# One written order for all engines in a four-layer attention kernel: keys' features in three steps, rows normalised two segments ahead

## The chip, the cores and the metric

The kernel runs on one core of a Trainium2 chip. The metric is the device time of one execution in microseconds (us), lower is better. A core has five engines that take their instructions in order, each from its own queue: TensorE (PE in the profile; PEld is its weight load), VectorE (DVE), ScalarE (ACT), GpSimd (POOL), and SyncE (SP), which here only starts transfers (DMAs). They wait for each other by semaphores, which the compiler sets where one instruction reads what another has written, or takes over its buffer.

## The reference, cut

Four layers of two kinds, A, B, A, B, over 2048 rows of 512 numbers, 32 heads of 16. Each layer is `x + layer(layernorm(x))`, and both layers of a kind share their weights.

```python
def _A_ref(x, wqkv, w_phi, wo):                    # linear attention
    q, k, v = heads(x @ wqkv)
    phi = lambda u: concat(softmax(u @ w_phi), softmax(-(u @ w_phi)))   # per head, 16 -> 32
    kv, z = sum_s phi(k)[s] v[s], sum_s phi(k)[s]
    o = phi(q) kv / (phi(q) z + 1e-6)
    return o @ wo

def _B_ref(x, wq, wk, wv, wo, beta):               # four segments of 512 rows
    for s in range(4):
        a_dot = causal_softmax(q_s k_s^T / 4) v_s
        a_mem = phi(q_s) M / (phi(q_s) z + 1e-6)   # phi(t) = t + 1 if t > 0 else exp(t)
        o_s = g * a_mem + (1 - g) * a_dot          # g = sigmoid(beta)
        M, z = M + phi(k_s)^T v_s, z + sum phi(k_s)
    return o @ wo
```

## The kernel before

**Products.** Everything is float32. The large products run on TensorE in three matmuls each: both operands are split into a rounded part `hi` and a rest `lo`, and hi*hi, hi*lo and lo*hi are summed (`mm3`, L418). So a product of 128 rows with a 512x512 matrix is 12 matmuls into a tile of 128x512 in PSUM, the accumulators' memory. Such tiles come from a pool `g` of three buffers; two larger ones, `lg` and `mx`, have one buffer each.

**A linear layer (A)** has two passes. `pass1` (L639) goes through four segments of 512 rows in the order 1, 2, 3, 0 (`SEGS`). For a segment:

- `norm_T` (L391) loads four tiles of rows, computes their moments on DVE (`moments`, `guard`), the inverse root on ACT by Ln and Exp (`root`) and sharpens it in six small instructions (`refine`, on DVE, or on POOL where `off` is set); ACT normalises each tile in place (`normal`), and `columns` transposes it on TensorE, ACT copying `hi` and DVE subtracting `lo`. With `slow` this is a generator of 15 steps, 11 of them up to the last normalisation.
- `v_tile` (L476) makes the values: four tiles, each a projection (12 matmuls) and a copy on ACT.
- `kproj` (L663), one for each of four tiles of keys: a projection, ACT's copy of it, then the features: largest and smallest of each head (`extremes`, DVE), differences to them (two instructions on POOL, `differences`), `exp` on ACT, sums, reciprocal and half of a scaling on DVE, the other half on POOL (`scale_k`). These differences, and the weights of the keys, already contain `w_phi`.
- `qproj` (L677): a projection, its copy, extremes, and a store; the features are made in the second pass.
- `kv` (L695): 32 matmuls add features-times-values of two tiles into `kva`, in buffer `lg` for tiles 0 and 1, `mx` for 2 and 3.

In segment n the loop at L735 takes a step of `k0 q0 k1 q1 v0 k2 q2 k3 q3 v1` and then one of `side`: the next segment's `norm_T`, then its values. Features of a key tile are all issued at once, behind its projection. In the last segment, features are issued in separate steps (L747 to L771). `pass2` (L781) computes the queries' features, products with `kva`, the division and the output projection with a residual, 16 tiles.

**The first layer** also has `first` (L572), which loads weights, multiplies `w_phi` into them on TensorE (`folded`) and makes segment 1's `norm_T` far enough that its rows are normalised; and beside its `pass1` runs `prepare` (L299, driver L1250), which splits 20 pieces of layer B's and output weights (a load, casts on ACT, subtractions on POOL) and stores both parts in DRAM (`kept`), from where `load_w` and `bring` (L235) read them later, two transfers of 1 MB for each matrix.

**A softmax layer (B)** is `steps` (L1114): a loop over numbered steps, with tables written by hand (`FIRST`, `GAPS`, `LAST`, `FINAL`, and `BEFORE` for the steps ahead of the first segment) that say at which step which projection, transposition, load or piece of another layer is issued. `opening` (L1096) loads the first weights and rows and sets constant rows of the operand tiles (`start`, L832, four fills); the driver (L1256) interleaves it with the first 76 steps (`A20`) of the linear layer's second pass before it. The rest of that pass is handed to `steps` as `side`, up to an amount of TensorE work `LEFT`. Layer 2's `steps` takes in turn the beginning of layer 3's `pass1` as `after`: the first segment's rows and values in the table `LAST`, and at L1226 to L1233 three steps of its first key projections, while layer 2's last tiles are added up (`end`, L1085).

**What sets the order.** The program is written by generators; what a scheduler then makes of it depends on flags. Instructions of DVE, ACT, POOL and SP go through `Ordered`, matmuls and transpositions through `held`:

```python
                j = (ends if ordered[0] or back[0] else floor).get(self.engine)
                if j is not None:
                    behind(i, j)
...
        if strict[0] and last[0] is not None:
            behind(i, last[0])
```

`behind` fixes that one instruction follows another on its engine without a wait. With `ordered` and `strict` set, an engine takes its instructions as written: so in `first`, in the last segment of each `pass1` and through the second pass and `steps`. Elsewhere, in segments 0 to 2 of `pass1` and at the very end of `steps`, a scheduler orders instructions within what the data allow, by its own forecast of the time.

Of the kernel before, what the change touches and what calls it, by code (L numbers as in the profile page):

```python
# [15 lines left out]
D = 512  # L16
# [21 lines left out]
LEFT = 44000  # L38
BEGIN = -31
MAXIMA = -9  # L40
A20 = 76
PREP = 6
EVERY = (2, 2)
# [57 lines left out]
          -18: "n", -17: "v2 n", -16: "n", -15: "n n", -14: "q1 n", -13: "n", -12: "v3 n", -11: "n", -10: "k1 n",  # L101
# [4 lines left out]
def interleave_kernel(ctx, tc, x_in, a_wqkv, a_wphi, a_wo, b_wq, b_wk, b_wv, b_wo, b_beta,  # L106
# [25 lines left out]
    strict = [False]  # L132
    last = [None]
    ordered = [False]
    back = [False]
    ends = {}
    floor = {}
    put_off = [None]

# [13 lines left out]
    class Ordered:  # L153


# [3 lines left out]
        def __getattr__(self, op):  # L159
            f = getattr(self.engine, op)  # L160

            def call(*a, **k):
                i = f(*a, **k)  # L163
# [9 lines left out]
    def held(i):  # L173

        if strict[0] and last[0] is not None:
            behind(i, last[0])
# [122 lines left out]
    def prepare():  # L299


        for _ in range(PREP):
            yield
        back[0] = True
        constants()
        back[0] = False
        for m, src in enumerate((b_wq, b_wk)):
            for kc in range(NC):
                raw = T2("xr", 3)
                sync.dma_start(out=raw, in_=src[kc * P : (kc + 1) * P, :])  # L310
                hi = T2("oh", OO, F32R)
                lo = T2("ol", OO, F32R)
                for e in range(2):
                    for r in range(2):
                        rv = raw.rearrange("p (c f r e d) -> p e r c d f", c=NC, f=2, r=2, e=2)[:, e, r]
                        hv = hi.rearrange("p (c f e d r) -> p e r c d f", c=NC, e=2, f=2, r=2)[:, e, r]
                        lv = lo.rearrange("p (c f e d r) -> p e r c d f", c=NC, e=2, f=2, r=2)[:, e, r]
                        back[0] = True
                        act.copy(hv, rv)
                        back[0] = False  # L320
                        pool.tensor_tensor(out=lv, in0=rv, in1=hv.bitcast(F32), op=SUB)
# [972 lines left out]
```

## Time and profile before

| | |
|---|---|
| median of 3 runs | 1601.99 us (1600.36 to 1604.97) |
| the profiled execution's own time | 1601.45 us |
| its span, from first to last instruction | 1599.7 us |
| TensorE busy with matmuls | 1512.0 us, 95% of the span |
| DVE / ACT / POOL busy | 1135.5 / 786.5 / 642.9 us (71% / 49% / 40%) |
| mean granted clock of TensorE | 0.989 of full speed |
| moved by DMA | 195.70 MB, mean 122 GB/s |

Every line of the trace says at what time (us from the span's start) which engine ran what, written as `out<-in` by the tiles' names. Matmuls stand at L185 and transpositions at L189, all recorded instructions of the other engines at L163, since helpers issue them: so they are told apart by tiles. Names in the first passes: `x` rows, `st` their statistics, `xr` and `oh`/`ol` the weights of `prepare`, `hh`/`hl` the columns, `g` a projection's accumulator, `U` a key projection's copy, `tb` a query's, `mm` extremes, `P` (or `e`) features, `es` their sums, `mx` and `lg` the accumulators of `kv`, `v` the values. In a row of one instruction or a run of like ones, the first number is its start, the second its duration together, `xN` their count, and what stands in brackets is the idle time before and what ended it. In a table of windows the columns are the window, its length, the busy time of PE, PEld, DVE, ACT and POOL with the number of instructions, the granted clock, and the mean busy share and GB/s of the DMA engines. A clock of 0.5 means that matmuls take twice as long.

### The profile page before, as it was taken

What the parts mean: (1) busy time and instruction counts of PE and PEld (TensorE: products, weight loads), DVE (VectorE), ACT (ScalarE), POOL (GpSimd) and SP (SyncE); (2) the same over time, 40 slices, a digit from 0 to 9 for tenths busy, and PEclk for the clock granted to TensorE, in tenths of its full rate; (3) what the DMA queues carried; (4) which work ended last, traced back from release to release, by engine and by line L of the source; (5) the groups of instructions that cost most, each with busy time, mean ns of one, the idle gap of its engine ahead of it and who ended that gap; (6) DMA issues with size and microseconds to landing.
All of it is one profiled execution on the core that took longest, in us unless ns stands there. A gap on an engine that the chain in (4) does not pass through costs nothing.

```text
span 1599.7 us, 28160 instructions
## 1 busy us (share of the span) xinstructions
PE 1512.0 (95%) x9856; PEld 1079.1 (67%) x9856; DVE 1135.5 (71%) x3282; ACT 786.5 (49%) x1178; POOL 642.9 (40%) x976
## 2 busy tenths in 40 slices
PE   7999998988999999999999999889889999999998
PEld 6788887765666666666568888777656666666554
DVE  4675775667787887888655657647688778777784
ACT  5444333425565565555534424343455655655553
POOL 1457653413443453433222337433234444533422
PEclk9999999999999999999999999999999999999999
DMA  7348144634443543543232111743354344334331
GB/s 273 132 137 264 73 163 151 185 95 148 132 106 100 140 100 106 140 105 122 81 144 61 52 58 51 236 152 106 103 176 113 103 137 106 102 111 107 81 88 52
DMA packets 100988, 195.70 MB, mean 122 GB/s; under 512 B 13552, under 2 KB 26992, under 8 KB 97776
## 3 DMA queue, kind: packets, MB, share of 16 engines
q1 hardware_dynamic: 99696, 193.38, 40.3%
q8 instruction: 79, 1.29, 0.3%
q10 hardware_dynamic: 1152, 0.52, 0.1%
q14 instruction: 61, 0.50, 0.1%
HBM read 101.05 MB, written 39.85 MB: 88 GB/s over the span
## 4 chain that ended last, share of the span: by engine, by line
PE 67%; DVE 17%; ACT 5%; issue 5%; DMA 3%; POOL 2%; SPq 1%; DVEq 0%; ACTq 0%; POOLq 0%
PE g L185 39%; DVE mx L163 9%; PE mx L185 8%; PE lg L185 8%; PE pv L185 6%; PE g L189 6%; ACT P L163 2%; ACT tb L163 2%; DVE mxs L163 2%; POOL P L163 1%; DVE ta L163 1%; DMA x<-x 1%; DVE es L163 1%; DMA xr<-in 1%; ACT x L163 1%
## 5 line engine op out<-in xcount | busy, mean ns | idle before, releaser
L163 DVE CUSTOM_DVE_ANT_0 mx<-mx,mask 128x128 f32<-128x128 f32 (+3 forms) x1024 | 510.4, 498 | 166.0 <-PE mx L185 131.4
L163 ACT ACTIVATE P<-lg 128x1024 f32<-128x1024 f32 x320 | 328.7, 1027 | 185.6 <-PE lg L185 172.7
L163 POOL TENSOR_SCALAR_AFFINE_SELECT P<-P 128x256 f32<-128x256 f32 (+1 forms) x448 | 190.3, 439 | 439.3 <-ACT P L163 437.6
L185 PE MATMUL g<-hh,wqk 128*128 128x512 f32 x512 | 180.6, 407 | 1.8 <-ACT hh L163 1.3
L185 PE MATMUL mx<-e,e 63*128 63x256 f32 (+2 forms) x1024 | 155.6, 360 | 22.0 <-DVE mxs L163 15.8
L185 PE MATMUL lg<-e,e 64*128 64x256 f32 (+2 forms) x1024 | 168.6, 387 | 8.0 <-ACT P L163 7.1
L185 PE MATMUL g<-w,oh 128*128 128x512 f32 x512 | 172.7, 420 | 3.6 <-ACT oh L163 2.7
L185 PE MATMUL pv<-P,v 128*32 128x512 f32 (+3 forms) x2048 | 165.2, 441 | 0.0
L185 PEld LDWEIGHTS lg<-e,e 64*128 64x128 f32 x1024 | 81.2, 184 | 103.6 <-issue 53.8
L185 PE MATMUL g<-w,hh 128*128 128x512 f32 x448 | 145.9, 406 | 3.1 <-ACT tb L163 3.1
L163 DVE DVE_READ_ACCUMULATOR2_ANT mxs<- 128x1 f32 x1024 | 144.5, 141 | 0.0
L185 PEld LDWEIGHTS mx<-e,e 63*128 63x128 f32 x1024 | 82.9, 185 | 70.4 <-DVE mxs L163 49.8
L185 PEld LDWEIGHTS pv<-P,v 128*32 128x32 f32 x2048 | 53.6, 109 | 98.7 <-issue 88.1
L185 PEld LDWEIGHTS g<-hh,wqk 128*128 128x128 f32 x512 | 96.3, 188 | 23.2 <-ACT hh L163 1.8
L185 PEld LDWEIGHTS g<-w,oh 128*128 128x128 f32 x512 | 91.7, 194 | 26.8 <-ACT oh L163 4.1
L163 POOL TENSOR_SCALAR tb<-tb 128x512 f32<-128x512 f32 x48 | 71.5, 1489 | 84.7 <-ACT tb L163 84.7
L185 PE MATMUL g<-w,ol 128*128 128x512 f32 x256 | 103.3, 404 | 1.1 <-DVE ol L163 1.1
L185 PE MATMUL g<-hl,wqk 128*128 128x512 f32 x256 | 100.3, 392 | 0.4 <-DVE hl L163 0.4
L163 ACT CAST ta<-g 128x512 fp32r<-128x512 f32 x64 | 37.4, 585 | 119.4 <-PE g L185 116.4
L185 PEld LDWEIGHTS g<-w,hh 128*128 128x128 f32 x448 | 80.0, 189 | 22.2 <-ACT tb L163 5.2
L185 PE MATMUL g<-w,hl 128*128 128x512 f32 x224 | 88.5, 395 | 0.0
L163 POOL TENSOR_TENSOR P<-P,rr 128x512 f32<-128x512 f32 x32 | 34.6, 1082 | 127.3 <-DVE rr L163 127.3
(133 smaller groups left out, 2714.3 us busy)
## 6 DMA issues: line engine op xcount, KB each, us to landing
e<-ta SPq DMA_DIRECT2D x384, 128.0 KB
wqk<-wqk SPq DMA_DIRECT2D x64, 512.0 KB
x<-x SPq DMA_DIRECT2D x48, 256.0 KB
xr<-in SPq DMA_DIRECT2D x28, 256.0 KB
pq<-tb SPq DMA_DIRECT2D x24, 256.0 KB
tb<-pq SPq DMA_DIRECT2D x24, 256.0 KB
x<-xr SPq DMA_DIRECT2D x24, 256.0 KB
xr<-x SPq DMA_DIRECT2D x24, 256.0 KB
```

What stands on the lines that cost most here:

```text
L163: i = f(*a, **k)
L185: return held(nc.tensor.matmul(*a, **k))
L189: return held(nc.tensor.transpose(*a))
```

## The change

It gives every engine one written order from the first instruction to the last, and rewrites what the scheduler had ordered:

- **Order.** `Ordered` and `held` always tie an instruction to the one written before it on its engine; the flags `ordered`, `strict`, `back` and `floor` are gone.
- **First passes, keys.** In segments 0 to 2 the steps are `k0 k1 q0 q1 k2 v0 k3 q2 q3`, and the features of a key tile are issued in three parts: extremes and differences behind its own projection, exp a projection later, the scaling another one later. `kv(1)` of a segment is issued behind `k0` of the next one (`late`).
- **Rows.** `upcoming(n)` opens the `norm_T` of segment n, always `slow` and with `refine` on POOL. In segment n, the side work is: the columns of segment n + 1, its values, then the rows of segment n + 2 up to their normalisation (`rows`, 11 steps).
- **Second `pass1`.** The queries' weights (`awq`) are loaded from the fifth step on, no longer behind the first segment's keys; side work waits until layer 2 has ended, and the features of the keys that are projected before that are put in a list (`aside`) and issued after `end`.
- **`prepare`.** The constants come first; then 44 pieces go through a cast on ACT, a subtraction on POOL and a store, each in a slot of its own, one slot later than the one before, with rows of weights asked for up to three ahead.
- **Weights and openings.** A kept matrix is loaded in eight transfers of 256 KB, two a step, for two of 1 MB. The four fills of `start` are issued one a step, `opening` takes other steps of the second pass, 82 of its steps precede `steps` (76 before), `LEFT` is 40000 (44000), and in `BEFORE` the projections `k1` and `v3` change places.

```diff
-LEFT = 44000
+LEFT = 40000
-A20 = 76
+A20 = 82
-EVERY = (2, 2)
+EVERY = 2
...
-          -18: "n", -17: "v2 n", -16: "n", -15: "n n", -14: "q1 n", -13: "n", -12: "v3 n", -11: "n", -10: "k1 n",
+          -18: "n", -17: "v2 n", -16: "n", -15: "n n", -14: "q1 n", -13: "n", -12: "k1 n", -11: "n", -10: "v3 n",
...
-                j = (ends if ordered[0] or back[0] else floor).get(self.engine)
-                if j is not None:
-                    behind(i, j)
+                if self.engine in ends:
+                    behind(i, ends[self.engine])
...
-        if strict[0] and last[0] is not None:
+        if last[0] is not None:
...
-            for t, k in zip((hi, lo), kept[key]):
-                dma(t, k)
+            for kc in range(NC):
+                for t, k in zip((hi, lo), kept[key]):
+                    dma(t[:, kc, :], k[:, kc, :])
                 yield
...
+        copied, stored = None, None
+        for piece in chain(pieces(), (None, None)):
+            if stored:
+                _, keep, tiles = stored
+                for k, t in zip(keep, tiles):
+                    dma(k, t.rearrange("p (c x) -> p c x", c=NC) if len(k.shape) == 3 else t)
+            if copied:
+                (raw, hi, lo), _, _ = copied
+                pool.tensor_tensor(out=lo, in0=raw, in1=hi.bitcast(F32), op=SUB)
+            if piece:
+                (raw, hi, _), _, _ = piece
                 act.copy(hi, raw)
+            copied, stored = piece, copied
+            for _ in range(EVERY):
+                yield
...
+            def upcoming(n):
+                h = []
+                spare = ("e8" if first else "w8") if n % 2 else None
+                return h, norm_T(self.xsrc, SEGS[n], h, spare, slow=True, off=True)
+            def rows(g):
+                for _ in range(11):
+                    next(g)
+                    yield
...
                     act.copy(pk, po)
-                    mm = extremes(pk, T2("mm", 2, shape=(P, 2, H)))
-                    if e is None:
-                        f = differences(pk, mm)
-                        exp(f)
-                        es.append(scale_k(f))
+                    mm = T2("mm", 2, shape=(P, 2, H))
+                    def features():
+                        e[t] = differences(pk, extremes(pk, mm))
+                    if aside[0] is None:
+                        features()
                     else:
-                        e[t] = differences(pk, mm)
+                        aside[0].append(features)
...
-                    steps = "k0 q0 k1 q1 v0 k2 q2 k3 q3 v1"
...
-                    for i, _ in enumerate(go(steps)):
-                        next(side, None)
+                    side = [] if n or first else [rows(g)]
+                    side += [g, v_tile(hTs, wv, vv, ("g", G))]
+                    if n + 2 < NSEG:
+                        upc = upcoming(n + 2)
+                        side.append(rows(upc[1]))
+                    side = chain(*side)
+                    def go(late):
+                        ready, done = [], []
+                        for step in "k0 k1 q0 q1 k2 v0 k3 q2 q3".split():
+                            if step == "v0":
+                                yield from kv(0)
+                                continue
+                            t = int(step[1])
+                            yield from (kproj if step[0] == "k" else qproj)(t, e)
+                            if done:
+                                es.append(scale_k(e[done.pop()]))
+                            if ready:
+                                exp(e[ready[0]])
+                                done.append(ready.pop())
+                            if step[0] == "k":
+                                ready.append(t)
+                            if step == "k0" and late:
+                                yield from late
+                    for i, _ in enumerate(go(late)):
+                        if i == 4 and n == 0 and not first:
+                            wq = load_w("awq", None, "e8")
+                        if aside[0] is None and i > 3:
+                            next(side, None)
...
-            self.start()
-            for _ in range(10):
-                yield
-                next(self.norm0)
+            fills = self.start()
+            for n in (0, 0, 1, 1, 1, 1, 1, 1, 0, 1, 1, 1, 1):
+                yield
+                next(fills, None)
+                for _ in range(n):
+                    next(self.norm0)
...
+            aside[0] = []
             next(after, None)
...
             self.end(o)
-            strict[0] = False
+            for f in aside[0]:
+                f()
+            aside[0] = None
...
-            if k >= 30 and k % 3 == 0:
+            if k % 3 == 0 and (5 < k < 24 or k > 41):
```

More of the change, by code (lines that the diff above doesn't have):

```diff
@@ L299, in prepare @@
     def prepare():
+        yield from constants()
         for _ in range(PREP):
             yield
[L304 to L321, printed above, removed]
-                        for _ in range(EVERY[m]):
-                            yield
-                for a, t in enumerate((hi, lo)):
-                    dma(wqk[m][:, :, a, kc, :], t.rearrange("p (c x) -> p c x", c=NC))
@@ L613, in first @@
             next(kfold)
-            side = norm_T(self.xsrc, SEGS[1], nxt, "e8", slow=True, off=True)
-            next(side)
+            upc = upcoming(1)
+            next(upc[1])
             for kc in range(NC):
@@ L712, in kv @@
                     yield
[L714 to L716 removed]
                 if n < NSEG - 1:
[L719 to L736 removed]
+                    if n == 0 and not first:
+                        upc = upcoming(1)
+                        next(upc[1])
```

98 lines of the change are left out of this document (42 added, 56 removed).

## The prediction, made before the changed kernel had run

> **What bounds the kernel now.** I read the page first (engine shares, the chain that ended last), then windows of the trace over the two first linear passes, then TensorE's rows in order of time, looking only at idle time, then the groups of rows by shape for the durations.
>
> ```profile
> span 1599.7 us, 28160 instructions
> PE 67%; DVE 17%; ACT 5%; issue 5%; DMA 3%; POOL 2%; SPq 1%; DVEq 0%; ACTq 0%; POOLq 0%
> 36.00:205.00 169.00, 161.79 (x836) 136.49 (x835) 111.69 (x180) 73.06 (x133) 100.52 (x103) 0.97 0.45 148
> 820.00:985.00 165.00, 160.33 (x839) 135.12 (x838) 107.14 (x189) 59.63 (x92) 63.35 (x59) 0.98 0.16 54
> ```
>
> The chain is TensorE's for two thirds. In the windows (columns: length, busy PE, PEld, DVE, ACT, POOL, granted clock, DMA share) TensorE works 161.8 of 169 us in layer 1's first pass and 160.3 of 165 in layer 3's. All that a better order can win there is some 12 us of idle time and the clock that is lost after it. DVE, ACT and POOL have a third or more of their time free, so they bound nothing by their sums; what can bound is the order in which they get to their work. The idle time that the change can reach is in these rows:
>
> ```profile
> 41.65 0.66 PE L189 MATMUL g<-ident,x 128*128 128x128 f32 x4 [2.16 <-DVE e L163]
> 87.94 4.67 PE L185 MATMUL mx<-v,P 128*128 128x68 f32 x30 [2.08 <-DVE P L163]
> 135.80 0.73 PE L185 MATMUL g<-w,hh 128*128 128x512 f32 x2 [2.23 <-ACT tb L163]
> 244.58 1.98 PE L185 MATMUL g<-KN,P 128*128 128x68 f32 x8 [2.05 <-DVE xr L163]
> 827.38 1.08 PE L189 MATMUL g<-ident,tmp 128*128 128x128 f32 x4 [2.86 <-ACT P L163]
> 829.13 2.07 PE L185 MATMUL g<-w,oh 128*128 128x512 f32 x4 [0.67 <-ACT oh L163]
> 1026.65 1.98 PE L185 MATMUL g<-KN,P 128*128 128x68 f32 x8 [2.75 <-DVE xr L163]
> 90.00:97.00 7.00, 7.00 (x30) 6.11 (x28) 5.81 (x11) 2.05 (x4) 2.50 (x6) 0.51 0.13 38
> 136.00:140.00 4.00, 4.00 (x25) 3.45 (x25) 3.86 (x6) 3.40 (x6) 3.18 (x3) 1.00 1.02 345
> 244.00:251.00 7.00, 6.42 (x20) 5.47 (x21) 6.72 (x16) 0.00 (x0) 1.99 (x2) 0.53 1.00 259
> 827.00:835.00 8.00, 6.95 (x26) 5.71 (x27) 7.44 (x16) 2.39 (x6) 2.59 (x2) 0.57 0.14 50
> 1026.00:1033.00 7.00, 6.35 (x21) 5.36 (x22) 6.62 (x17) 0.07 (x1) 2.25 (x3) 0.56 0.94 249
> ```
>
> A wait costs twice: four of them are followed by about 7 us at a granted clock near 0.5 (3.4 us lost each), the one at 135.80 by none.
>
> **The change part by part.** Durations (mean ns), from layer 1's first pass:
>
> ```profile
> 79.10 2.96 PE L185 MATMUL g<-w,e 128*128 128x512 f32 x12
> 81.90 2.44 PE L185 MATMUL g<-e,e 128*128 128x512 f32 x10
> 139.10 3.46 PE L185 MATMUL mx<-v,P 128*128 128x68 f32 x30
> 25.80 1.55 PE L189 MATMUL g<-ident,P 128*128 128x128 f32 x12
> L163 ACT ACTIVATE P<-P 128x1024 f32<-128x1024 f32 x18 | 19.1, 1063 | 12.9 <-POOL P L163 12.8
> L163 ACT CAST oh<-xr 128x128 fp32r<-128x128 f32 x32 | 11.4, 434 | 0.0
> L163 ACT COPY tb<-g 128x512 f32<-128x512 f32 x15 | 8.8, 587 | 20.1 <-PE g L185 19.5 <-ACT oh L163 0.6
> L163 ACT ACTIVATE x<-x,st 128x512 f32<-128x512 f32 x8 | 5.9, 806 | 0.5 <-DVE st L163 0.5
> L163 ACT ACTIVATE st<-st 128x4 f32<-128x4 f32 x4 | 0.8, 212 | 2.6 <-DVE st L163 2.5
> L163 DVE TENSOR_REDUCE es<-P 128x64 f32<-128x1024 f32 x18 | 21.7, 1208 | 3.5 <-ACT P L163 3.5
> L163 DVE TENSOR_REDUCE mm<-U 128x32 f32<-128x512 f32 x32 | 20.4, 676 | 22.7 <-ACT U L163 22.5
> L163 DVE TENSOR_TENSOR P<-P,es 128x512 f32<-128x512 f32 x16 | 16.9, 1059 | 0.4
> L163 DVE RECIPROCAL es<-es 128x64 f32<-128x64 f32 x16 | 8.7, 544 | 0.3
> L163 DVE BATCH_NORM_STATS2 bs<-x 128x6 f32<-128x512 f32 x6 | 3.9, 677 | 0.4 <-DMA x<-in 0.4
> L163 DVE BATCH_NORM_AGGREGATE st<-bs 128x2 f32<-128x6 f32 x6 | 0.9, 168 | 0.0
> L163 DVE TENSOR_SCALAR st<-st 128x4 f32<-128x4 f32 x6 | 1.8, 299 | 0.1
> L163 POOL TENSOR_TENSOR P<-P,es 128x512 f32<-128x512 f32 x16 | 21.7, 1356 | 15.3 <-DVE es L163 15.2
> L163 POOL TENSOR_TENSOR P<-U,mm 128x512 f32<-128x512 f32 x16 | 18.4, 1148 | 27.0 <-DVE mm L163 27.0
> 28.54 0.49 POOL L163 TENSOR_TENSOR st<-st 128x4 f32<-128x4 f32 x2 [6.79 <-ACT st L163]
> 29.97 0.24 POOL L163 TENSOR_SCALAR st<-st 128x4 f32<-128x4 f32 x1
> 37.72 1.47 SPq L163 DMA_DIRECT2D x<-in  x2
> 40.31 0.69 DVE L163 BATCH_NORM_STATS2 bs<-x 128x6 f32<-128x512 f32 x1 [0.85 <-DMA x<-in]
> 52.74 1.04 DVE L163 TENSOR_SCALAR eb<-eb 128x32 f32<-128x32 f32 x1
> ```
>
> A projection of 12 matmuls takes 2.80 us alone (79.10 to 81.90), an outer product `kv` of 32 about 3.5, the transposition of a tile 0.5. A copy is 0.59, a pair of extremes 1.35, sums and reciprocal 1.75, DVE's half of a scaling 1.06, POOL's 1.36, a key's two differences 2.2, statistics of a tile 0.85, their guard 0.3, a normalisation 0.81, a cast for the stored weights 0.43, exp 1.06. `refine` on POOL, six small instructions, took 1.67 (28.54 to 30.21), and a load of rows landed 2.6 after its issue (37.72, 40.31). TensorE gets no work added; all that counts is who waits.
>
> *The waits that I expect to be new.* In the changed program's order, the next-but-one segment's rows are worked on in the last projections k3, q2, q3 of a segment, where no value projection runs beside them, so TensorE needs 2.80 us for each; then comes k0 of the next segment and at once `kv(1)`, which reads the features of k2 and k3. Their last step stands behind the rows' work on in-order engines.
>
> W1, layer 1, segment 1 to 2. From the last matmul of q2: its copy 0.59, extremes 1.35, sums and reciprocal of k2 1.75, POOL's half 1.36, `refine`, which stands behind it on POOL, 1.67; then on ACT three normalisations and two casts 3.29, behind which stands q3's copy 0.59; extremes 1.35, sums and reciprocal of k3 1.75, POOL's half 1.36: 15.1 us. TensorE has q3 and k0, 5.6. That is 9.5 of waiting. And q2's copy is itself late: ahead of it on ACT stands the Ln of the rows' variances, which waits on DVE for k3's extremes and three tiles of statistics, 0.59 + 1.35 + 2.55 + 0.3 = 4.8 after k3's end; Ln, Exp and a cast bring it to 5.7, 2.9 later than q2's end at 2.8. W1 = 12.4. The rows' loads are past a queue too: on SP they stand behind a load of weights that waits for POOL's piece behind k2's differences, 0.59 + 0.68 + 2.24 + 1.34 = 4.9 after k2's end; with `kv(0)` and two and a half projections' worth of matmuls (9.1) between k2's end and k3's they land about 1 us ahead of k3's end, so I add nothing; where they land later, W1 grows by as much.
>
> W2, segment 2 to 3: here the first normalisation stands ahead of q2's copy. From k3's end: copy 0.59, one extreme 0.68, differences 2.24, a piece of weights on POOL 0.67, `refine` 1.67, normalisation 0.81, q2's copy 0.59: 7.25; exp, three normalisations, two casts 4.35, q3's copy 0.59, then 1.35 + 1.75 + 1.36: 16.65. TensorE has 8.4. W2 = 8.3. W5 is the same place in layer 3, without casts and pieces: 15.2, W5 = 6.8.
>
> W3, layer 3, first segment: k0's and k1's extremes are set aside until the layer before has ended. From its last matmul DVE has the last addition 0.7, four extremes 2.7, four tiles of statistics 3.4, guard 0.3, q0's extremes 1.35, sums and reciprocal 1.75; POOL 1.36 and `refine` 1.67; ACT 0.81: 14.0, while TensorE stands at the first transposition after 33 matmuls (7.7). Wait 6.3. Then normalisation, q1's copy, extremes, sums and reciprocal, POOL's half: 19.9, against 15.7 (three matmuls and two transpositions on). Wait 4.2. W3 = 10.5. That `awq` is loaded from k1 on, 2 MB in eight pieces, costs at most 1 us, taken as nothing: at the 345 GB/s of the window from 136 it needs 6 us, the layer's last products cover most of it, and q0 starts with the first two pieces.
>
> W4, behind it: the next rows' statistics, `refine` and normalisations stand between q3 and k0's copy. From q3's end: copy, extremes, k3's scaling 4.75 (by then the rows have landed), statistics and guard 3.7, Ln and Exp 0.42, `refine` 1.67, four normalisations 3.24, k0's copy 0.59: 14.4. TensorE has the last values, k0, `kv(1)` and two transpositions, 10.1, and then all three projection buffers are full: 4.3. The next buffer waits for k0's extremes and a subtraction, 1.3 more. W4 = 5.6.
>
> Sum of the new waits 43.6. For the clock behind them the trace gives 0 to 3.4 each; I take 2.6, nearer the four that lost 3.4, since all five are longer but swallow part of the slow stretch: 13.0. The Trainium skill ("TensorE: Matmul & The Clock Gate", Part 1) says that a free-running window of about 3.4 us without work halves the clock and one of work restores it. The trace disagrees on the start (2.08 us was enough) and agrees on the length; by one window at half speed the loss would be 1.7 each, 8.5, and the time some 4.5 us lower.
>
> *What goes.* The waits at 87.94, 135.80, 827.38 and 829.13, whose covers are the three steps and, in layer 3, the extremes set aside: 7.9, with two slow stretches, 6.8: -14.7. What is late next there is W1 to W3. The wait at 41.65 gives way to another: the constants' DVE work (52.74 and what follows it), some 3.3, now stands ahead of k0's extremes, and these ahead of the transposed rows that free the buffers; about 2.7 for 2.16, +0.5.
>
> *Opening of layers 2 and 4.* Weights in eight pieces, fills one at a time, begun earlier: at 244.58 and 1026.65 the residual came late behind 2 MB of weights, fills and rows at a DMA share of 1.00 and 0.94. At most 4.8 of waits and 6.8 of clock can go, and at least nothing, since the same bytes now move beside the same residual loads. I take half: -5.8. The six more steps of the second pass ahead of layer 2 and the smaller share later cancel (the same matmuls), and in the table v3 and k1 change places, 12 matmuls against 12. The stored weights' cast, subtraction and store, now in three slots, cost nothing beyond W1 and W2: POOL is busy 100.5 of 169.
>
> Sum: 43.6 + 13.0 - 14.7 + 0.5 - 5.8 = +36.6 on the profiled execution's 1601.45 us (span 1599.7, the rest around it; the runs' median is 1601.99): **1638 us**.
>
> **The rivals.** *Hidden* (faster): the point is W1's: if q3's scaling chain ends within TensorE's 5.6 us, as it does in each pass's last segment, where no rows are prepared, nothing new waits. Then -14.7 and -5.8 to -11.6: 1575 to 1581. For it: a third of DVE and more of ACT is free. Against it: the chain needs 15.1 through queues that take their work in order. *Work only*: the engines pass the rows in gaps and only DVE's own sum counts behind k3: W1 5.0, W2 and W5 3.3, W3 6.4, W4 none, 18.0; with 6.8 of clock, 18.0 + 6.8 + 0.5 - 14.7 - 5.8 = +4.8: 1606. *Worse*: a cast that waits for its weight rows holds the copies behind it on ACT; this row gives the size:
>
> ```profile
> L163 ACT CAST oh<-xr 128x512 fp32r<-128x512 f32 x12 | 7.4, 622 | 10.1 <-DMA xr<-in 9.7 <-ACT oh L163 0.3
> ```
>
> All of the 9.7 on TensorE's path and the full clock loss (17.0) make 1652. *Does nothing*: the later parts already had a written order; gains and waits cancel within 0.3%, about what a measurement of this kernel can tell: 1601.
>
> **How the numbers follow.** Forecast 0.63, hidden 0.13, work only 0.13 (a quarter of it within 0.3%), worse 0.07, nothing 0.04. Slower 0.80, the same 0.07, faster 0.13. The range runs from work only, 1604, to a little past worse, 1658; it leaves out hidden, nothing and the ends, 0.2.
>
> **What would show it.** In TensorE's rows of the changed kernel: `mx<-v,P` near 80 us with some 12 us of idle time ended by DVE or POOL on `P`, and near 130 with 8; in layer 3 a transposition `g<-ident,x` with 6 and `lg<-v,P` with 4 soon after the layer's end; a projection with 4 to 6 some 25 us on; `mx<-v,P` again with 7. Behind each, rows of clock near 0.5. The waits at 87.94, 827.38 and 244.58 gone or shorter. If `mx<-v,P` shows no wait over 3 us, the chains above are wrong, and the time is that of hidden or work only.

## The result, and the profile after

The changed kernel takes **1651.27 us** (median of 6 runs, 1648.24 to 1657.57), the kernel before 1604.32 beside it (6 runs, 1600.36 to 1608.13): 1.030 of the time before, 95% interval 1.0272 to 1.0328. It was forecast slower, 1638 us, within 1604 to 1658. The profiled execution took 1648.24, the shortest of the six.

First the page of the changed kernel, then windows with cuts that fall on the same matmuls in both kernels: to the first product of layer 1's second pass, to layer 2's last `pv` product, to the first product of layer 3's second pass, to the last matmul. After:

```profile
span 1646.1 us, 28161 instructions
PE 64%; DVE 19%; issue 5%; ACT 5%; POOL 3%; DMA 2%; SPq 1%; ACTq 0%; POOLq 0%; DVEq 0%
0.00:236.73 236.73, 199.71 (x1001) 167.97 (x1001) 123.46 (x207) 93.67 (x172) 111.00 (x136) 0.91 0.47 153
236.73:843.42 606.69, 581.97 (x4024) 393.36 (x4024) 448.19 (x1438) 319.31 (x462) 235.97 (x400) 0.99 0.45 128
843.42:1039.81 196.39, 176.70 (x858) 148.62 (x858) 110.68 (x175) 61.10 (x96) 70.89 (x80) 0.90 0.15 53
1039.81:1642.28 602.47, 574.18 (x3976) 385.28 (x3976) 447.43 (x1433) 313.38 (x450) 234.56 (x392) 0.99 0.41 117
```

The same four windows of the kernel before:

```profile
0.00:206.76 206.76, 188.99 (x1000) 160.64 (x1000) 129.67 (x219) 93.82 (x172) 108.63 (x124) 0.98 0.52 173
206.76:819.04 612.28, 584.37 (x4024) 394.43 (x4024) 447.38 (x1438) 318.37 (x462) 235.22 (x400) 0.99 0.44 128
819.04:988.20 169.16, 164.15 (x858) 138.11 (x858) 110.82 (x194) 61.66 (x96) 65.14 (x62) 0.98 0.17 58
988.20:1596.02 607.82, 574.45 (x3976) 385.94 (x3976) 446.89 (x1433) 312.62 (x450) 233.89 (x391) 0.99 0.41 117
```

The matmuls are the same, row for row (the first number in brackets counts them; the one more in the first row lies on the cut). Both first passes grew, by 30.0 and 27.2 us; the rest, openings and layer B, shrank by 5.6 and 5.4: +46.3 in sum, the spans' 46.4. Length less busy PE is TensorE's idle time: in the two first passes it grew by 19.2 and 14.7 (33.9), and busy PE by 10.7 and 12.6 (23.3) at a granted clock of 0.91 and 0.90 where it was 0.98. In windows of 0.25 us, TensorE's busy time times what the clock lacks of 1 comes to 28.2 us in these two passes and to 8.2 before. So 34 us are waits, 20 are the same matmuls at half clock, and 3 of the busy time stay unexplained.

TensorE's rows of the changed kernel with more than 1 us of idle time in the two first passes:

```profile
42.64 0.66 PE L184 MATMUL g<-ident,x 128*128 128x128 f32 x4 [1.06 <-DVE e L159]
82.93 0.67 PE L180 MATMUL mx<-v,P 128*128 128x68 f32 x2 [2.42 <-POOL P L159]
92.46 3.26 PE L180 MATMUL mx<-v,P 128*128 128x68 f32 x14 [8.85 <-POOL P L159]
144.69 0.69 PE L180 MATMUL mx<-v,P 128*128 128x68 f32 x2 [4.84 <-POOL P L159]
148.72 1.55 PE L180 MATMUL mx<-v,P 128*128 128x68 f32 x6 [3.33 <-POOL P L159]
183.29 1.65 PE L180 MATMUL g<-w,e 128*128 128x512 f32 x3 [4.78 <-ACT tb L159]
866.44 1.12 PE L184 MATMUL g<-ident,x 128*128 128x128 f32 x4 [5.93 <-ACT x L159]
872.30 3.26 PE L180 MATMUL lg<-v,P 128*128 128x68 f32 x14 [2.28 <-POOL P L159]
909.94 1.12 PE L184 MATMUL g<-ident,x 128*128 128x128 f32 x4 [3.93 <-ACT x L159]
956.95 0.70 PE L180 MATMUL mx<-v,P 128*128 128x68 f32 x2 [3.50 <-POOL P L159]
960.57 3.26 PE L180 MATMUL mx<-v,P 128*128 128x68 f32 x14 [2.93 <-POOL P L159]
```

Five places are those of the prediction: W1 at 82.93 and 92.46 (two waits, since `kv(1)` starts with k2's features and then needs k3's), W2 at 144.69 and 148.72, W3 at 866.44 and 872.30, W4 at 909.94, W5 at 956.95 and 960.57. The sixth, at 183.29, it did not have. W1's chain can be read off the other engines, in order of time:

```profile
76.56 0.40 DVE L159 TENSOR_SCALAR st<-st 128x4 f32<-128x4 f32 x1
77.57 0.62 ACT L159 COPY tb<-g 128x512 f32<-128x512 f32 x1
84.53 0.81 ACT L159 ACTIVATE x<-x,st 128x512 f32<-128x512 f32 x1 [5.39 <-POOL st L159]
87.11 0.61 ACT L159 COPY tb<-g 128x512 f32<-128x512 f32 x1
87.75 1.28 DVE L159 TENSOR_REDUCE mmq<-tb 128x32 f32<-128x512 f32 x2 [5.81 <-ACT tb L159]
90.83 1.58 POOL L159 TENSOR_TENSOR P<-P,es 128x512 f32<-128x512 f32 x1 [4.43 <-DVE es L159]
```

It runs zigzag: the rows' guard on DVE, then Ln, Exp and q2's copy on ACT, k2's scaling on POOL (81.36) with `refine` behind it, the normalisations on ACT that waited 5.39 us for it, then q3's copy, q3's extremes on DVE, only then k3's sums (88.95), and POOL's half, at whose end (92.41) the product goes on. DVE, ACT and POOL each stand still for 4 to 6 us at a time in it. The price in clock stands behind it:

```profile
83.00:92.00 9.00, 0.60 (x2) 0.41 (x2) 4.18 (x7) 4.86 (x10) 3.53 (x9) 0.50 0.69 238
92.00:104.00 12.00, 11.54 (x51) 10.88 (x52) 3.25 (x6) 2.41 (x5) 5.36 (x10) 0.52 0.78 294
104.00:112.00 8.00, 8.00 (x38) 6.52 (x36) 2.19 (x4) 3.69 (x7) 3.91 (x5) 1.00 0.11 47
```

While TensorE waits, the low clock costs nothing. But it stays at 0.52 for 12 us after work is back, 5.8 us lost, where the wait of 2.08 us in the kernel before lost 3.4.

### The profile page after: what moved, and what is told of

The parts are those of the page before. It is cut to its first block, busy times and chain, and to the rows that moved or that the text cites. A ratio compares the mean times of both kernels' runs of the same rounds, so it can differ in the third digit from the quotient of the medians.

```text
span 1646.1 us, 28161 instructions
## 1 busy us (share of the span) xinstructions
PE 1532.6 (93%) x9856; PEld 1095.2 (67%) x9856; DVE 1130.5 (69%) x3252; ACT 787.4 (48%) x1178; POOL 652.4 (40%) x1006
## 4 chain that ended last, share of the span: by engine, by line
PE 64%; DVE 19%; issue 5%; ACT 5%; POOL 3%; DMA 2%; SPq 1%; ACTq 0%; POOLq 0%; DVEq 0%
PE g L180 36%; DVE mx L159 8%; PE mx L180 8%; PE lg L180 7%; PE pv L180 6%; PE g L184 6%; POOL P L159 2%; DVE es L159 2%; ACT P L159 2%; ACT tb L159 2%; DVE mxs L159 1%; DVE bs L159 1%; DVE mmq L159 1%; DVE ta L159 1%; DMA ot<-in 1%
## 5 line engine op out<-in xcount | busy, mean ns | idle before, releaser
L180 PE MATMUL g<-w,oh 128*128 128x512 f32 x512 | 168.4, 410 | 2.5 <-ACT oh L159 2.1
L159 DVE TENSOR_REDUCE mmq<-tb 128x32 f32<-128x512 f32 x64 | 40.9, 680 | 72.1 <-ACT tb L159 72.1
L159 POOL TENSOR_TENSOR P<-P,es 128x512 f32<-128x512 f32 x32 | 49.1, 1533 | 102.4 <-DVE es L159 102.1
```

The source lines that it names most:

```text
L180: return held(nc.tensor.matmul(*a, **k))
```

## The experiments

Twelve kernels were run, each timed against the kernel before on the same chip, whose median lay at 1602 to 1606 us in all of them. The theory: the written order makes chains that zigzag between in-order queues, with the rows' work and the queries' copies and extremes ahead of the keys' last step. Rivals: the early place of `kv(1)`, the pieces of stored weights, the features set aside at layer 2's end.

**Values last.** The rows are worked on earlier, ahead of the values.

```diff
-                    side += [g, v_tile(hTs, wv, vv, ("g", G))]
+                    side.append(g)
                     if n + 2 < NSEG:
                         upc = upcoming(n + 2)
                         side.append(rows(upc[1]))
+                    side.append(v_tile(hTs, wv, vv, ("g", G)))
```

> The changed kernel, with one edit: in segments 0 to 2 the side work is columns, then the rows two segments ahead, then the values (the change has the values ahead of the rows). So the rows are worked on beside k1, q0 and q1, and the value projections stand beside k3, q2 and q3, which gives TensorE about 5.6 us for each of these instead of 2.8. Theory (the rows' work stands between q2's and q3's copies in the engines' queues, and TensorE has nothing else to do there): the waits at 82.93 and 92.46 (11.3 us together), 144.69 and 148.72 (8.2), 956.95 and 960.57 (6.4) and 909.94 (3.9) go or stay under 1 us each, 29.8 in all, and with them about 19 us of half clock: about 1602 us. Rival (kv(1) right behind k0 comes too early for a feature chain in three steps, wherever the rows are): 2 to 4 us stay at each of the three places, with a slow stretch behind each: about 1625. Rival (the rows are only moved to another place where they hold something, now the queries' copies beside k1 to q1): new waits of like size on g, about 1640 to 1650.

1667.95 us, 1.0412 of the time before (1.0377 to 1.0446). TensorE's rows:

```profile
64.08 3.26 PE L180 MATMUL lg<-v,P 128*128 128x68 f32 x14 [8.13 <-POOL P L159]
96.37 1.78 PE L180 MATMUL mx<-v,P 128*128 128x68 f32 x14 [1.06 <-POOL P L159]
944.79 3.26 PE L180 MATMUL lg<-v,P 128*128 128x68 f32 x14 [8.59 <-POOL P L159]
```

The waits on `mx` shrank as the theory said (8.85 to 1.06), but the same wait now stands ahead of the first product, on `lg`, three times over 8 us (8.47 at 127.47 is the third): it went where the rows went. At the two other places 2.48 and 2.43 us stayed on `mx`, as the first rival said of all three. The second rival was right in kind, a new wait where the rows are now, though on `lg` and not on `g`, and 18 us longer than it said. So the features come late where the rows' work stands beside a query's projection, in both places that were tried.

**Product later.** `kv(1)` a projection later.

```diff
-                            if step == "k0" and late:
+                            if step == "k1" and late:
```

> The changed kernel, with one edit: a segment's second product kv(1) is issued behind k1 of the next segment, not behind k0, so TensorE has one projection (2.8 us) more to do while the features of k2 and k3 are made. Theory (the chain of the features ends at a time that TensorE's own later work does not change): each of the three waits on mx shrinks by 2.8, to about 8.5, 5.4 and 3.6; the slow clock behind them shrinks little; 8.4 us less, 1641 to 1643. Rival (k1's copy and extremes get into the queues ahead of the late features, so the product waits as long as before): 1650. Rival (the product needs only to come after k0's own features): the waits go as a whole, near 1605.

1647.33 us, 1.0281 (1.0241 to 1.0321): hardly other than the change. None of the three expectations: the waits on `mx` are gone, and the time is not won.

```profile
88.23 1.11 PE L184 MATMUL g<-ident,x 128*128 128x128 f32 x4 [6.52 <-ACT tb L159]
150.74 1.12 PE L184 MATMUL g<-ident,x 128*128 128x128 f32 x4 [5.39 <-DVE e L159]
```

The next columns wait for a buffer instead. In the first row q3's copy, behind the normalisations, frees it late. The second has another cause: `e` is here the columns' rest, and the columns' casts stand on ACT behind a cast for the stored weights, which waits until a store has left its buffer:

```profile
148.86 0.62 ACT L159 CAST oh<-xr 128x512 fp32r<-128x512 f32 x1 [8.47 <-DMA wqk<-oh]
```

The early product was where the delay showed, not where it came from; and with it later, the stored weights hold TensorE too.

**Longer slots** for the stored weights, for the wait at 183.29.

```diff
-EVERY = 2
+EVERY = 3
```

> The changed kernel, with one constant: EVERY 3 for 2, so a piece of the stored weights is cast every three steps of the first pass. For the wait that the prediction didn't have, 4.78 us at 183.29 in the last segment: q's copy stands on ScalarE behind a cast that waits until the store of the piece three before has left its buffer (7.43 us idle ahead of the cast at 182.13). Theory (three buffers, and only one slot of time between that store's issue and the cast): with longer slots this wait goes, and with it 3 us of half clock; those at 82.93 to 148.72 change by under 1.5 us in sum, since rows and features and not the pieces hold them: about 1643. Rival (pieces make up a good part of the waits at 92.46 and 148.72 too, by casts and subtractions in the same queues): these fall by 3 or more, 1635 or less. Rival (the cast waits for GpSimd's subtraction, which stands behind the scaling of keys in any case): the wait stays, 1651.

1666.09 us, 1.0404 (1.0367 to 1.0441). The waits of W1 and W2 stayed (1.90 and 8.81, 3.67 and 3.59), so the pieces' spacing does not make them. The wait at 183.29 went. But pieces were left for the end of the last segment, and there it came back larger, behind casts that waited 3.46 and 8.11 us for their stores:

```profile
214.75 5.33 PE L180 MATMUL g<-e,e 128*128 128x512 f32 x12 [5.35 <-ACT U L159]
231.59 6.67 PE L180 MATMUL lg<-v,P 128*128 128x68 f32 x30 [11.01 <-POOL P L159]
```

**A step's shift** for the same wait, so that the casts change places with the copies.

```diff
-PREP = 6
+PREP = 7
```

> The changed kernel with one constant: PREP 7 for 6, which moves each piece of the stored weights by one step against the projections, so that on ScalarE a cast no longer stands directly ahead of a projection's copy but behind it. The longer slots did not settle the wait of 4.78 us at 183.29; they moved pieces into the last segment and made such waits longer. Theory (the copy is held by the cast ahead of it, which waits for the store of the piece three before): the wait at 183.29 goes and with it about 3 us of clock, the others stay: 1642 to 1646. Rival (the wait of the cast comes round from one projection to the next, through extremes, scaling, subtraction and store, wherever the cast stands): a wait of 3 to 5 stays near there, 1651.

1653.16 us, 1.0302 (1.0270 to 1.0335). The rival was right: 3.93 us stay at 182.57, 2.69 more stand at 171.25. In that kernel's rows the round can be followed:

```profile
170.62 0.58 ACT L159 COPY tb<-g 128x512 f32<-128x512 f32 x1
174.30 1.58 POOL L159 TENSOR_TENSOR P<-P,es 128x512 f32<-128x512 f32 x1 [7.17 <-DVE es L159]
175.84 2.54 POOL L159 TENSOR_TENSOR ol<-xr,oh 128x512 fp32r<-128x512 f32 x2
179.63 0.47 SPq L159 DMA_DIRECT2D bwv<-ol  x1
181.41 0.62 ACT L159 CAST oh<-xr 128x512 fp32r<-128x512 f32 x1 [8.25 <-DMA bwv<-oh]
```

A query's copy, its extremes, the key's sums behind them, POOL's scaling, the subtractions behind that, the store, the cast that wants the store's buffer, and behind it the next query's copy (181.94): 11.3 us a round. The cast is one link; another is again that the key's sums stand behind the query's extremes.

**Nothing aside.**

```diff
-            aside[0] = []
...
-            for f in aside[0]:
-                f()
-            aside[0] = None
```

> The changed kernel without the list aside: the features of layer 3's first keys, and the statistics of the next rows, are issued where they are written, between layer 2's last additions, no longer behind them. Theory (the wait of 5.93 at 866.44 is a chain that begins with layer 2's last matmul, with eight extremes and statistics on DVE that now come earlier): the waits at 866.44 and 872.30, 8.2 us together, fall to 2 or less, and the half clock of 17 us behind them goes; layer 2's last additions come at most 3 us later, which TensorE doesn't see, as it has layer 3's projections to do: 1637 to 1641. Rival (the wait is made by the loads, rows behind 2 MB of the queries' weights): no change at that place, 1650. Rival (the additions that come later hold layer 2's end and TensorE's accumulators): a wait of 2 to 4 us moves into the end, as the 3.5 us of before at 827.38 and 829.13: 1645.

1651.79 us, 1.0310 (1.0278 to 1.0342): no change. The wait of 5.93 us shrank to 1.23, but 3.14 came at 868.63, for a query's copy, and 2.89 on `mx` at 904.33. So the list aside does make the wait at 866.44, and without it others come. Layer 3's first pass took 193.6 for 196.4 us, while layer 1's, which is the same code in both, took 240.1 for 236.7. What this part is worth is not settled; it is not the main thing.

**Features first, and rows unworked.** The two links of the zigzag taken out singly and together. The first edit issues a key's last step ahead of the projection's copy, not behind it:

```diff
-                            yield from (kproj if step[0] == "k" else qproj)(t, e)
-                            if done:
-                                es.append(scale_k(e[done.pop()]))
+                            for j, _ in enumerate((kproj if step[0] == "k" else qproj)(t, e)):
+                                if j == 3 and done:
+                                    es.append(scale_k(e[done.pop()]))
+                                yield
```

> The changed kernel, with one edit: a key's last step (sums, reciprocal, scaling) is issued ahead of the copy and the extremes of the projection beside it, not behind them. So k3's features no longer stand behind q3's extremes on DVE, nor these behind the normalisations on ScalarE. Theory (it is the order of the in-order queues, a zigzag of rows' work, query's copy, extremes and key's sums, that makes the features late): k3's features come when GpSimd has done refine and its half of the scaling, near 86 us in place of 92.4, so the waits at 82.93 and 92.46 shrink from 11.3 to about 5.4; those at 144.69 and 148.72 from 8.2 to about 4, at 956.95 and 960.57 from 6.4 to about 3; with some 7 us of clock about 1630. Rival (the queries' copies are as late as before, and what the product gains is waited for at the columns' buffers, as when kv(1) came behind k1): 1645. Rival (the rows' work fills the engines there, whatever the order): no change.

The second lets the rows of segments 2 and 3 be loaded and transposed, without the arithmetic between (`bare` for n > 1):

```diff
+        if bare:
+            for _ in range(10):
+                yield
+            hT[:] = htiles(spare)
+            for t in range(4):
+                columns(hT, t, xt[t])
+                yield
+            return
```

> The changed kernel without the arithmetic on the rows two segments ahead: in both linear layers, segments 2 and 3 of the first pass are loaded but their moments, root, refine and normalisation are left out, so their columns are of rows that are not normalised. Loads, steps and all else stay. Theory (this work, in the queues between q2's and q3's copies, is what makes the product wait; the three steps by themselves leave q3's copy 0.59, extremes 1.35, k3's sums and reciprocal 1.75 and GpSimd's half 1.36 against k0's 2.80 on TensorE, 2.3 us): the waits on mx fall from 11.3, 8.2 and 6.4 to 2.3 each or less, that at 909.94, where segment 1's rows are worked on too, from 3.9 to under 1; with the clock that goes with them 1610 to 1617. Rival (the three steps and the early kv(1) hold the product, rows or no rows): waits of 5 us and more stay, 1640.

Both together:

> The edits of the two runs before together: a key's last step ahead of the copy and extremes of the projection beside it, and the rows two segments ahead not worked on (moments, root, refine and normalisation of segments 2 and 3 in both first passes left out; the columns are of rows that are not normalised). The fourth corner of a square: as changed 1651, features first 1618, rows unworked 1627. Theory (either link alone leaves 3 to 4 us on mx: refine on GpSimd ahead of k3's half of the scaling with the one, q3's copy and extremes ahead of k3's sums with the other; with both gone k3's features take copy 0.59, extremes 1.35, differences 2.2, exp 1.06, sums and reciprocal 1.75 and GpSimd's 1.36 from k3's end, 8.3, and TensorE has q2, q3 and k0, 8.4): no wait over 1 us on mx, three times 3 to 4 us and their slow clock of 3 to 5 each less than with one edit: 1598 to 1604. Rival (some 3 us there are of kv(1)'s early place alone): waits near 3 stay, 1615.

| | rows worked | rows unworked |
|---|---|---|
| key's last step behind the copy | 1651.27, 1.0300 (1.0272 to 1.0328) | 1627.29, 1.0133 (1.0098 to 1.0169) |
| key's last step ahead of it | 1618.19, 1.0090 (1.0062 to 1.0119) | 1593.15, 0.9928 (0.9906 to 0.9950) |

The waits on `mx` in W1's and W5's places, with features first:

```profile
84.41 2.46 PE L180 MATMUL mx<-v,P 128*128 128x68 f32 x14 [3.98 <-POOL P L159]
927.75 2.47 PE L180 MATMUL mx<-v,P 128*128 128x68 f32 x13 [3.65 <-POOL P L159]
```

with the rows unworked:

```profile
83.27 3.09 PE L180 MATMUL mx<-v,P 128*128 128x68 f32 x14 [3.18 <-POOL P L159]
935.66 2.24 PE L180 MATMUL mx<-v,P 128*128 128x68 f32 x14 [3.19 <-POOL P L159]
```

and with both (0.96 at 125.46 is the next):

```profile
82.14 1.78 PE L180 MATMUL mx<-v,P 128*128 128x68 f32 x14 [0.80 <-POOL P L159]
```

Either link alone leaves 3 to 4 us (for rows unworked 2.3 or less had been expected), and with both out the product no longer waits to speak of. This shows the theory for the waits on `mx`. For the first link nothing was left out, so it is the order that counts. For the second the rows' work itself was left out, so the runs show that this work holds the product, not that it could be done in another order without doing so. Features first gains more than expected (33 us for some 21), since it also opens the round at 183.29, where 0.74 us are left, and takes away the 2.28 on `lg`. The rows gain less (24 us for 34 to 41): 3.18 us of waiting still bring a slow stretch, and while W4 goes, W3 and the round stay.

**Repairs together**: features first, `kv(1)` behind k1, nothing aside; and these with `refine` on DVE (`off=True` left out in `upcoming`).

> The changed kernel with three of the edits together: a key's last step ahead of the next copy, kv(1) behind k1, nothing set aside at layer 2's end. Nothing is left out. Theory (what waits on mx with features first, 3.98, 3.82 and 3.65, is under the 2.8 that k1 gives but for 1 us each; and with k0's and k1's extremes done earlier the wait of 4.39 at layer 3's first columns falls by the 2.5 that they took): 9 to 11 us of waits and 8 to 12 of clock less than 1618: 1596 to 1602, within 0.5% of the kernel before. Rival (kv(1)'s wait turns into one at the columns' buffers, since the queries' copies are late behind the normalisations, as it did when kv(1) alone was moved): 1610 to 1618.

> The three repairs, with refine of the upcoming rows on DVE, not on GpSimd, and nothing else changed. With the three repairs alone the product no longer waits, but TensorE stands 5.35 us at 85.77, 2.65 at 132.18 and 3.10 at 140.51 at the columns' buffers, since the copies of q3 and k0 come behind normalisations that waited 4.00 us on ScalarE for refine on GpSimd, where it stands behind a half of the scaling. Theory (that place in GpSimd's queue is the link that is left): normalisations and copies come some 3 us earlier in layer 1, its three waits fall from 11.1 to 3 to 5 us, layer 3's 8.17 at 885.65, where ScalarE waited only 1.77 for refine, by 1 to 2; with the clock 8 to 14 us less, 1606 to 1612. Rival (DVE's own queue is as long there: refine stands behind sums, scaling and extremes): waits within 2 us of these, 1615 to 1620. Rival (six small instructions ahead of k3's sums bring the wait on mx back): slower than 1620.

1619.70 us, 1.0095 (1.0066 to 1.0124), and 1618.32, 1.0092 (1.0061 to 1.0123). Both times a rival was right: no more than features first alone. The wait of 5.35 us at 85.77, with the three repairs, is this row with `refine` on DVE:

```profile
84.41 1.11 PE L184 MATMUL g<-ident,x 128*128 128x128 f32 x4 [4.58 <-ACT tb L159]
```

As long as q3's copy stands behind the normalisations, TensorE runs out of buffers there, whichever of the two engines refines. Two more waits stay that `refine` hardly changes: 3.10 us at 140.51 (4.36 at 141.03 with `refine` on DVE), behind the same kind of cast for the stored weights as with the later product, and in layer 3 the longest of all (7.67 with `refine` on DVE), at the columns of rows whose statistics wait for their load:

```profile
885.65 1.11 PE L184 MATMUL g<-ident,x 128*128 128x128 f32 x4 [8.17 <-ACT x L159]
```

**The openings on the kernel before**: the parts of the change that concern kept weights' pieces, `start`, `opening`, its steps, `A20`, `LEFT` and `BEFORE`, and nothing of the rest; and the eight pieces alone (the hunk of `bring`).

> The kernel before, with the change's openings alone: kept weights in eight pieces, fills one a step, the opening's other steps of the second pass, A20 82, LEFT 40000, k1 and v3 exchanged. The flags, the first passes and the stored weights' work stay as before. Theory (the openings' gain, 5.6 and 5.4 us between the traces from the start of the second pass to layer B's last product, is their own): 11 us faster, about 1592, with the waits on the residual at 244.58 and 1026.65 and the slow clock behind them gone. Rival (the gain comes from the written order ahead of the second pass, that is from what the first pass leaves in the queues): no change. Rival (the other order of the openings costs as much in the first steps of layer B as the residual's wait gives): 1600 to 1606.

> The kernel before, with kept weights loaded in eight transfers of 256 KB for two of 1 MB, and nothing else of the change. Theory (the residual at 244.58 and 1026.65 comes late because opening, fills, rows and weights are all asked for in the pass's last third, and the pieces' size matters little): no more than 3 us faster, 1600 to 1604. Rival (the two transfers of 1 MB are what the residual stands behind): both waits go with their slow clock, 8 to 11 us faster, 1592.

The openings alone: **1589.65 us** (8 runs, 1586.99 to 1597.48), 0.9903 (0.9878 to 0.9928), faster than both kernels. Their gain is their own. Against this kernel the rest of the change costs some 62 us, and some 29 with features first. The eight pieces alone: 1607.74 us, 1.0015 (0.9992 to 1.0038), no change. With them alone, what stood ahead of the pass's products at 244.58 is still there, as 2.13 us at 238.61 and this:

```profile
252.60 1.11 PE L185 MATMUL g<-KN,P 128*128 128x68 f32 x8 [2.85 <-DVE ot L163]
```

With the openings, TensorE's longest wait in that pass is 1.59 (the profile is that of the slowest of the eight executions):

```profile
231.75 0.66 PE L189 MATMUL g<-ident,tmp 128*128 128x128 f32 x4 [1.59 <-DVE ot L163]
```

So the size of the transfers alone does not do it. Which of the other edits carries it (the opening's steps, the fills, `A20` and `LEFT`, k1 and v3), and whether through when weights, fills and rows are asked for, was not tried singly.

No run keeps the new steps and leaves their order to the scheduler, or writes down the order that the scheduler had found. So the runs show what this written order costs, not that a written order must.

## Why the prediction was right, and where its terms were off

| step | predicted | measured |
|---|---|---|
| W1 | 12.4 | 2.42 + 8.85 = 11.3 |
| W2 | 8.3 | 4.84 + 3.33 = 8.2 |
| W3 | 10.5 | 5.93 + 2.28 = 8.2 |
| W4 | 5.6 | 3.9 |
| W5 | 6.8 | 3.50 + 2.93 = 6.4 |
| the round of cast and copy | in "worse" alone | 4.8 |
| wait at 41.65 | +0.5 | -1.1 |
| waits of before that go | -7.9 | -7.8 |
| sum of waits, first passes | +36.2 | +33.9 |
| clock, first passes | 13.0 - 6.8 = +6.2 | 28.2 - 8.2 = +20.1 |
| rest of TensorE's busy time, first passes | not in it | +3.2 |
| openings and layer B | -5.8 | -10.9 |
| sum | +36.6 | +46.3 |

- **The new waits** were right in place, order and size; W1 and W2 follow link by link. W1's first part, q2's copy late behind the Ln of the rows, is there too: q3's matmuls begin at 74.76, and q2's copy at 77.57, 2.8 later, for 2.9 forecast. W3 and W4 were 2 us shorter each than the sum of their links. That the sum of waits came out within 2.3 us is in part luck: the five places were 5.6 too long, and the round, 4.8, was not in it. "Work only", in which engines pass rows in gaps, is refuted.
- **The clock** is the term that was mis-sized. "I take 2.6, nearer the four that lost 3.4, since all five are longer but swallow part of the slow stretch": they swallow part of it, but the stretch is longer. The five places lost 5.8, 5.0, 6.5, 3.0 and 5.3 us, the round 2.7: 28.2 in sum, 4.7 each. The slow stretches of before that went (at 42, 90 and 827 us) had cost 1.7 + 3.4 + 3.1 = 8.2. The sentences of the Trainium skill ("TensorE: Matmul & The Clock Gate", Part 1: The HAM clock gate) would have made it worse: by an estimate from them, with one window of about 3.4 us of work to come back, each costs 1.7, and the time would be some 4.5 us lower still. The trace does not agree: in the rows at 92 to 104 the clock took more than three such windows of work to come back, and already the stretches of some 7 us in the kernel before were two.
- **The wait at 183.29** was missed in the sum. "Worse" had the mechanism, a cast that holds the copies behind it on ACT, with another cause (rows that come late, not a store that frees its buffer late) and the price 9.7, where it was 4.8. That its time, 1652, is all but the measured one is chance: its extra wait was twice too long, its clock term too low, and its openings gained too little.
- **The openings** gained 10.9, near the upper bound of 11.6, of which half had been taken; but not by its terms. The idle time fell by 8.3, where at most 4.8 had been allowed, since waits went that the prediction did not count, two in each opening. Of the clock, where 6.8 had been allowed, hardly anything was won: slow stretches cost 7.5 us in these parts before and 6.8 after, since short ones came at other places (at 301, 424, 1104 and 1226 us). Two of the uncounted waits, in the kernel before:

```profile
261.10 2.00 PE L185 MATMUL g<-KN,P 128*128 128x68 f32 x16 [2.00 <-ACT P L163]
294.70 0.66 PE L189 MATMUL g<-ident,tmp 128*128 128x128 f32 x4 [1.51 <-ACT tb L163]
```

- **Hidden** had a condition: that the last features are scaled within TensorE's 5.6 us. The square of four shows that it nearly holds when both links are out, and then the time is 1593, 12 us above 1581 even with the rows' work left out. In that profile W3's first wait stays, 4.41 us at 835.15, with 6.3 lost to the clock behind it, and 1.82 of the round.

So three errors partly cancel: the clock and the rest of TensorE's busy time 17 us too low, the openings 5 and the waits 2 too high.

## What to carry to other kernels

In a written order, follow a chain through the queues, not through the data: here a key's last step needed nothing from the query beside it, yet stood behind that query's extremes, these behind its copy, and the copy behind another segment's normalisations, and moving one line ahead of the copy won 33 us. When a wait is taken away and the time stays, as with the later product, look for where the same late instruction, or the one that was hidden behind it, is waited for next. And a wait on TensorE is to be priced with its slow clock, which here cost as much as two thirds of the waiting itself.

## What the runs showed of the hardware

The clock did not come back with the first work: after 8.85 us of waiting it stayed near 0.5 for 12 us, and in the kernel with unworked rows behind a wait of 3.18 us it stayed there for some 10 us (83 to 94). In windows of 0.25 us, the stretches at half clock within these kernels' spans are some 3.5, 7, 10.5, 14, 17 or 20.5 us long, the waiting itself included, so the loss came out in steps of 1.7 us (1.7, 3.4, 5.1, 6.8, 8.5 and 10.2). Their length did not follow the wait's. With the three repairs, a wait of 8.17 us (885.65) cost 2.4 us of TensorE's work; in the kernel with the openings alone, one of 2.09 (88.14) cost 5.1, where the same matmuls had cost 3.4 in the kernel before behind 2.08. Every stretch of 13 us or more holds small products of `kv`, and behind the wait of 8.17, where projections and transpositions follow, the clock was back after some 5 us; whether it is the kind of work that holds it down was not tried. Nor does a stretch need a wait of 2 us: one of 3.5 us came behind 1.46 us at 423.13 in the changed kernel, where the same wait in the kernel before (1.46 at 398.19) had none. Two profiles of the same code in layer 1 differed by 3.4 us (236.7 and 240.1), 2.9 of it by slow stretches, so differences of that size between single profiles say nothing here.
